# Eight short loads into a scratch tile, between the second and the third chunk of a streaming kernel

## The chip, the cores and the metric

The kernel runs on one core of a Trainium2 chip. The metric is device time in microseconds (us). Each time below is a median of several executions. All executions that were compared carry the label "fast", and the clock granted in them is 1.0 (full speed). A profile covers one execution, and its "span" is some 2 us shorter than the time.

## The reference

```python
# B, S, D = 512, 32, 640; x, fx and alpha are bfloat16, alpha has one element
def reference(x, fx, alpha):
    return x + alpha * fx
```

There is hardly any arithmetic. 41.9 MB have to be read and 21.0 MB written.

## The kernel before

The tensors are seen as 128 partitions of 163840 B each and cut into five chunks of 128 x 16384 elements (4 MB). Each chunk has a load of x, a load of fx, one VectorE (DVE) operation, and a store. All large transfers are issued by SP (SyncE) in the order of the program; alpha is loaded by ACT. A tile framework puts in the semaphores and their waits; the program order is kept as written. A semaphore is a counter that a transfer raises when it has landed, and for which an instruction can wait.

```python
    def load_x(k):
        xt[k] = xs.tile([P, CHUNK], x.dtype, tag="x", name="x_t")      # 4 buffers
        nc.sync.dma_start(out=xt[k][:], in_=xv[:, bass.ts(k, CHUNK)])

    def load_f(k):
        ft[k] = fs.tile([P, CHUNK], fx.dtype, tag="f", name="f_t")     # 2 buffers
        nc.sync.dma_start(out=ft[k][:], in_=fxv[:, bass.ts(k, CHUNK)])
    ...                                # compute(k): x_t = f_t * alpha + x_t on DVE; store(k): x_t to out
    load_x(0)
    load_f(0)
    load_x(1)
    load_f(1)
    load_x(2)
    compute(0)
    load_f(2)
    store(0)
    load_x(3)
    compute(1)
    load_f(3)
    store(1)
    ...                                # on in the same way; the last chunk is computed and stored in halves
```

I write x(k), f(k) and store(k) for the transfers of chunk k.

## Time and profile before

| | before |
|---|---|
| time | 152.69 us (152.47 to 152.9) |
| span of the profiled execution | 150.6 us |
| bytes moved, mean rate | 62.92 MB, 418 GB/s |
| DMA queue 1, share of 16 engines | 98.0% |
| DVE busy | 58% |

These lines are from the page of the kernel before. The "DMA" row gives the busy share of the 16 DMA engines in 40 equal slices of the span, in tenths (9 is 90% or more); the last line gives packets, megabytes and the share of 16 engines' span.

```profile
span 150.6 us, 85 instructions
DVE  0000009999679998499991006999900089997000
DMA  6999999999999999799999999999999999999994
q1 hardware_dynamic: 2304, 62.92, 98.0%
```

The DMA engines have work from the first slice to the last. In the trace nearly every 32 KB packet (one row of a chunk) takes 1.213 us on its engine, and 16 x 32768 B / 1.213 us is 432 GB/s. The Trainium skill, page "DMA: Bandwidth & Descriptors", section "Where 436 GB/s comes from", gives 435 GB/s as the ceiling of the fabric and says that between HBM and SBUF the HBM side, about 358 GB/s, is what binds; the trace fits the first figure and not the second (432 GB/s in the packets, 418 GB/s over the span, with one core at work). DVE keeps waiting for data (49.5 us in all).

The timeline of the kernel before: start, duration (both us), engine, source line, operation, output and input. "SPq" is the issue of a DMA by SP, not the transfer. The brackets give the idle time before an operation and what ended it.

```profile
0.73 0.38 SPq L59 DMA_DIRECT2D x_t<-in_x_dram  x1
2.10 0.57 SPq L63 DMA_DIRECT2D f_t<-in_fx_dram  x1
2.71 0.48 SPq L59 DMA_DIRECT2D x_t<-in_x_dram  x1
22.84 17.28 DVE L69 SCALAR_TENSOR_TENSOR x_t<-f_t,a_f,x_t 128x16384 bf16<-128x16384 bf16 x1 [20.57 <-DMA f_t<-in_fx_dram]
40.16 0.33 SPq L63 DMA_DIRECT2D f_t<-in_fx_dram  x1
42.25 17.28 DVE L69 SCALAR_TENSOR_TENSOR x_t<-f_t,a_f,x_t 128x16384 bf16<-128x16384 bf16 x1 [2.12 <-DMA f_t<-in_fx_dram]
62.24 17.28 DVE L69 SCALAR_TENSOR_TENSOR x_t<-f_t,a_f,x_t 128x16384 bf16<-128x16384 bf16 x1 [2.71 <-DMA f_t<-in_fx_dram]
```

The issue at 2.71 us is x(2): five transfers of 9.7 us each are queued by 3.2 us. The DVE starts mark when f(0), f(1) and f(2) have landed, within a tenth of a us. f(2) is issued at 40.16 us, when the first DVE operation has set its buffer free; x(2) has then not even begun to move, so the queue does not run empty.

### The profile page before, as it was taken

Reading aid. Unit: us, or ns where it says so; the run is one execution under the profiler, and the core shown is the slowest. Engines: PE = TensorE matmul, PEld = TensorE weight load, DVE = VectorE, ACT = ScalarE, POOL = GpSimd, SP = SyncE. Lnnn points to the kernel's source line nnn. Section 1 sums busy time; section 2 is a strip of 40 time slices with the busy share of each in tenths; the row PEclk is TensorE's granted clock in tenths of the full one; section 3 lists DMA queues with packets and bytes.
Section 4 is the critical chain, followed back from the end, with each engine's and each line's share of the span. In section 5 each row is a group of like instructions: output and inputs, shape, how many; then the busy total and the mean of one; then the engine's idle time right before and its main releaser. Section 6 shows DMA issues by size and latency. Waiting matters only on the chain.

```text
span 150.6 us, 85 instructions
## 1 busy us (share of the span) xinstructions
PE 0.2 (0%) x1; PEld 0.1 (0%) x1; DVE 86.9 (58%) x8; POOL 0.2 (0%) x4
## 2 busy tenths in 40 slices
PE   0000000000000000000000000000000000000000
PEld 0000000000000000000000000000000000000000
DVE  0000009999679998499991006999900089997000
POOL 0000000000000000000000000000000000000000
DMA  6999999999999999799999999999999999999994
GB/s 200 444 453 435 418 418 418 418 444 453 444 453 435 418 418 418 339 444 470 418 418 418 418 418 435 435 435 453 426 435 444 418 418 435 435 435 405 426 444 205
DMA packets 2306, 62.92 MB, mean 418 GB/s; under 512 B 258, under 2 KB 258, under 8 KB 258
## 3 DMA queue, kind: packets, MB, share of 16 engines
q1 hardware_dynamic: 2304, 62.92, 98.0%
q10 hardware_dynamic: 2, 0.00, 0.0%
HBM read 41.94 MB, written 20.97 MB: 418 GB/s over the span
## 4 chain that ended last, share of the span: by engine, by line
DMA 56%; DVE 29%; DVEq 6%; issue 0%; SPq 0%
DMA f_t<-in_fx_dram 56%; DVE x_t L69 29%; DVEq L131 6%; SPq L59 0%; DVEq L69 0%
## 5 line engine op out<-in xcount | busy, mean ns | idle before, releaser
L69 DVE SCALAR_TENSOR_TENSOR x_t<-f_t,a_f,x_t 128x16384 bf16<-128x16384 bf16 (+1 forms) x6 | 86.6, 14439 | 49.5 <-DMA f_t<-in_fx_dram 49.5
L26 DVE COPY a_f<-a_ps 128x1 f32<-128x1 f32 x1 | 0.2, 159 | 1.1 <-PE a_ps L24 1.1
L22 DVE MEMSET ones<- 1x128 bf16 x1 | 0.2, 165 | 0.8 <-PEq L120 0.8
L24 PE MATMUL a_ps<-a,ones 1*128 1x1 bf16 x1 | 0.2, 159 | 1.9 <-DMA a<-in_alpha_dram 1.9
L120 POOL MEMSET const-bfloat16-1.0<- 128x1 bf16 x1 | 0.1, 102 | 0.0
L120 POOL MEMSET const-uint8-127<- 128x1 uint8 x1 | 0.1, 102 | 0.0
L24 PEld LDWEIGHTS <-ones 1*128 1x128 bf16 x1 | 0.1, 100 | 1.0 <-DVE ones L22 1.0
L120 POOL MEMSET const-float32-0.0<- 128x1 f32 x1 | 0.1, 99 | 0.2 <-issue 0.2
L120 POOL MEMSET const-float32-1.0<- 128x1 f32 x1 | 0.1, 99 | 0.0
## 6 DMA issues: line engine op xcount, KB each, us to landing
x_t<-in_x_dram SPq DMA_DIRECT2D x5, 4096.0 KB, 34.8
f_t<-in_fx_dram SPq DMA_DIRECT2D x5, 4096.0 KB, 32.1
out_dram<-x_t SPq DMA_DIRECT2D x4, 4096.0 KB, 36.5
out_dram<-x_t SPq DMA_DIRECT2D x2, 2048.0 KB, 15.2
a<-in_alpha_dram ACTq DMA_DIRECT2D x1, 0.0 KB
```

Of the source, the lines that this page charges most:

```text
L22: nc.vector.memset(ones[:], 1.0)
L24: nc.tensor.matmul(a_ps[:], ones[:], a_1[:], start=True, stop=True)
L26: nc.vector.tensor_copy(out=a_f[:], in_=a_ps[:])
L69: nc.vector.scalar_tensor_tensor(out=xt[k][:, s], in0=ft[k][:, s], scalar=a_f[:], in1=xt[k][:, s], op0=ALU.mult, op1=ALU.add,)
L120: nc = _bacc.Bacc("TRN2", target_bir_lowering=False, num_devices=1)
L131: with _tile.TileContext(nc) as tc:
```

## The change

It adds eight loads of 15 down to 2 rows (512 to 736 B each) into a scratch tile that nobody reads. The output is the same.

```diff
     load_x(1)
     load_f(1)
+    m_t = consts.tile([16, 8 * 512], x.dtype, name="m_t")
+    for i, n in enumerate([15, 14, 12, 10, 8, 6, 4, 2]):
+        w = 256 + 16 * i
+        nc.sync.dma_start(out=m_t[:n, i * 512 : i * 512 + w], in_=xv[:n, :w])
     load_x(2)
     compute(0)
     load_f(2)
```

I call the eight loads m0 to m7. The diff does not show which semaphores the framework gives out. The built program's own list of SP's instructions with their waits does (an output of the build, not a profile):

```
L59 DMACopy x_t_77<-in_x_dram 128x16384                            # x(0)
L63 DMACopy f_t_79<-in_fx_dram 128x16384                           # f(0)
L59 DMACopy x_t_81<-in_x_dram 128x16384                            # x(1)
L63 DMACopy f_t_83<-in_fx_dram 128x16384                           # f(1)
L92 DMACopy m_t_85<-in_x_dram 15x256                               # m0
L92 DMACopy m_t_85<-in_x_dram 14x272                               # m1
L92 DMACopy m_t_85<-in_x_dram 12x288                               # m2
L92 DMACopy m_t_85<-in_x_dram 10x304 [waits DMAHW0_49]             # m3: alpha's
L92 DMACopy m_t_85<-in_x_dram 8x320 [waits DMAHW1_49]              # m4: x(0)'s
L92 DMACopy m_t_85<-in_x_dram 6x336 [waits DMAHW2_49]              # m5: f(0)'s
L92 DMACopy m_t_85<-in_x_dram 4x352 [waits DMAHW3_49]              # m6: x(1)'s
L92 DMACopy m_t_85<-in_x_dram 2x368 [waits DMAHW4_49]              # m7: f(1)'s
L59 DMACopy x_t_94<-in_x_dram 128x16384 [waits DMAHW5_49]          # x(2): m0's
```

(The comments are mine.) The DMAs take their completion semaphores in rotation from eight, over SP and ACT together, and an issue waits until the last user of its semaphore is complete. Alpha's load, on ACT, has the first of the eight. In the kernel before, x(2) was the sixth DMA and had no wait.

## The prediction

> **What bounds the kernel now.** DMA bandwidth, from start to end. The page shows 62.92 MB over a span of 150.6 us (418 GB/s), queue 1 busy 98.0% of 16 engines' span. A 32 KB row packet takes 1.213 us in the trace (16 x 32768 B / 1.213 us = 432 GB/s); the 4 MB transfers land every 9.7 us in issue order. DVE is busy 58% and only waits (49.5 us for f_t). The last half store is issued at 138.3 us and lands only at the end, so a backlog stands even there. Whatever leaves the DMA queue empty, or adds bytes, goes into the time whole.
>
> **What the change adds.** Eight loads, 71 rows of 512 to 736 B, about 42 KB: below 0.2 us over 16 engines. Nobody reads the tile. Eight issues of 0.33 to 0.57 us each (SP's issues in the timeline) would be harmless: five 4 MB transfers are queued by 3.2 us, worth 50 us.
>
> **What the change moves.** This is the cost. In the built program the DMAs take their completion semaphores in rotation from eight, and its listing of waits shows that an issue waits for the previous user of its semaphore. Before, x(2) was the sixth DMA and waited for nothing (issued 2.71 us). Now alpha, x(0), f(0), x(1), f(1), m0, m1, m2 take all eight, and m3 to m7 wait for alpha, x(0), f(0), x(1), f(1). m7 waits for f(1), which lands at 42.15 us, and x(2) stands behind m7 on SP (it also waits for m0, which lands just behind f(1)). The Trainium skill, "DMA: Bandwidth & Descriptors", section "Anatomy of one DMA", says that such waits are held by the issuing sequencer, not by the DMA engines; so SP sits until 42.2 us and the DMA queue runs dry behind f(1). Rotation by eight leaves later semaphores as before; later waits on short loads are long satisfied.
>
> **Cost.** m7 is issued at 42.2 (0.35 to 0.5 us), x(2) at about 42.65. From an empty queue x(0) took 12.3 us from issue to landing (0.73 to 13.0: 1.0 us to the first packet, first packets of 1.9 instead of 1.2 us). So x(2) lands at about 54.9 instead of 51.87: +3.0 us. f(2), store(0) and x(3) are issued within 2 us of x(2), and 40 us of transfers are then queued; f(3) is issued at 59.6 as before. No later gap absorbs the shift: nearly all 3.0 us arrive at the end.
>
> **Predicted time:** 155.7 us (+3.0 us, 2.0%), range 154.9 to 156.7 (8 in 10). Faster by over 2%: 1%; within 2%: 52%; slower by over 2%: 47%. It stands on the border.
>
> **What would show it.** The timeline: m4 to m7 issued at about 13, 22.7, 32.4 and 42.2 us, x(2) at 42.6. In the slices, one near 42 us with DMA at 2 to 5 tenths instead of 9. The DMA queue's waits: some 10 us each of short loads on x_t and f_t loads. The first two large DVE operations unmoved (22.84, 42.25), the third at about 65 instead of 62.24, everything after later by about 3 us. DVE busy 86.9 us unchanged.
>
> **What would make it wrong.** A warm queue restarting cheaper than x(0)'s start (+2 us); m0 landing late, or short transfers costing microseconds on engine 0 (+4 us or more); the first store's slow packets near 58 us (up to 1.99 us) changing.

## The result, and the profile after

| | before | after |
|---|---|---|
| time, first pair | 152.69 us (2 runs) | 156.53 us (156.5 to 156.55, 2 runs) |
| ratio, first pair | 1 | 1.0247 (95%: 1.022 to 1.0274) |
| time, second set (run e8_after_again) | 152.63 us (7 runs) | 156.05 us (155.69 to 156.33, 4 runs) |
| ratio, second set | 1 | 1.0196 (95%: 1.0145 to 1.0246) |
| span of the first profile | 150.6 us | 154.7 us |

A ratio is the mean time of one kernel's fast runs over the mean of the other's in the same rounds, so it is not quite the ratio of the medians. The change costs 3.4 to 3.8 us. The first pair lies above the 2% border with its whole interval; in the second set the interval holds 2%, so that set alone doesn't decide. The prediction had put the change on this border, with 155.7 us.

The same lines of the page of the changed kernel:

```profile
span 154.7 us, 93 instructions
DVE  0000009999499994099995003999910069998000
DMA  6999999999689999899999999999999999999993
q1 hardware_dynamic: 2446, 62.96, 96.3%
```

The DMA row has a dip (6 and 8) in the slices from 38.7 to 46.4 us. The row counts a packet in the slice where it starts. So does the view by windows, whose share can therefore exceed 1; its last two figures are the share of the 16 engines and GB/s. From 40 to 44 us, before and after:

```profile
40.00:44.00 4.00, 0.00 (x0) 0.00 (x0) 1.88 (x2) 0.00 (x0) 1.00 1.14 492
40.00:44.00 4.00, 0.00 (x0) 0.00 (x0) 1.89 (x2) 0.00 (x0) 1.00 0.75 240
```

The second, smaller dip (8, near 62 us) stands where the kernel before has its 7: it is there in both kernels.

The timeline of the changed kernel, cut around the issues of m4 to m7 (source line 92) and of what follows:

```profile
13.12 0.27 SPq L92 DMA_DIRECT2D m_t<-in_x_dram  x1
22.83 0.27 SPq L92 DMA_DIRECT2D m_t<-in_x_dram  x1
22.94 17.29 DVE L69 SCALAR_TENSOR_TENSOR x_t<-f_t,a_f,x_t 128x16384 bf16<-128x16384 bf16 x1 [20.48 <-DMA f_t<-in_fx_dram]
32.55 0.25 SPq L92 DMA_DIRECT2D m_t<-in_x_dram  x1
42.26 0.23 SPq L92 DMA_DIRECT2D m_t<-in_x_dram  x1
42.34 17.28 DVE L69 SCALAR_TENSOR_TENSOR x_t<-f_t,a_f,x_t 128x16384 bf16<-128x16384 bf16 x1 [2.11 <-DMA f_t<-in_fx_dram]
42.54 0.36 SPq L59 DMA_DIRECT2D x_t<-in_x_dram  x1
43.01 0.36 SPq L63 DMA_DIRECT2D f_t<-in_fx_dram  x1
65.92 17.29 DVE L69 SCALAR_TENSOR_TENSOR x_t<-f_t,a_f,x_t 128x16384 bf16<-128x16384 bf16 x1 [6.30 <-DMA f_t<-in_fx_dram]
```

m4 to m7 leave one by one as x(0), f(0), x(1) and f(1) land. x(2) is issued at 42.54 us instead of 2.71. Its own wait would have held it nearly as long: m0, whose semaphore it takes, was queued behind f(1) and landed only at 42.43 us (39.7 us after its issue), and m7's issue ended at 42.49 us. The runs don't tell these two waits apart; both end just behind f(1). The first two DVE operations have not moved by more than 0.1 us, and the third starts 3.68 us later (65.92 against 62.24). The waits of the DMA queue say the same (issuer, line, what it waited for: us in total, times, longest); first the changed kernel:

```profile
SPq L92 <- DMA f_t<-in_fx_dram: 18.9, 2, 9.4
SPq L92 <- DMA x_t<-in_x_dram: 18.1, 2, 9.4
```

The longest waits of SP in the kernel before were longer than these. They came with 4 MB transfers still queued on the engines:

```profile
SPq L80 <- DVE x_t L69: 55.5, 3, 28.7
SPq L63 <- DVE x_t L69: 41.6, 3, 17.4
SPq L63 <- DMA f_t<-in_fx_dram: 20.2, 2, 19.5
```

A long wait of SP is no loss in itself. It becomes one when the engines run out of what SP has issued already. The chain of work that ended last (start, duration, what) shows this for the changed kernel:

```profile
2.11 40.14 DMA f_t<-in_fx_dram
...
42.26 0.23 SPq L92
42.49 0.04 issue
42.54 0.36 SPq L59
...
43.01 22.82 DMA f_t<-in_fx_dram
```

Between two loads the chain now runs over SP's issue of a load that nobody needs (L92) and the issue of x(2) (L59). In the kernel before, SP appeared in this chain once, at the start; over the same stretch it ran

```profile
22.84 17.30 DVE x_t L69
...
40.16 21.99 DMA f_t<-in_fx_dram
...
62.24 17.29 DVE x_t L69
```

### Where the microseconds are

From the packets' starts and durations in the trace I add up, for each of the 16 engines on average: the time in which no large packet runs, and the time by which large packets exceed 1.213 us (0.611 us for the half rows of the last stores). "Again" is the second profile of each kernel, from the runs e9_before_again and e8_after_again.

| us per engine | before | before again | after | after again |
|---|---|---|---|---|
| idle behind f(1), 40 to 44 us | 0 | 0 | 2.28 | 2.24 |
| slower packets, 40 to 50 us | 0.01 | 0.01 | 0.71 | 0.63 |
| slower packets, 50 to 70 us (before the first store) | 0.88 | 0.81 | 1.27 | 1.39 |
| idle at the end, behind the first engine that is done | 0.42 | 0.95 | 0.97 | 1.04 |
| span | 150.6 | 151.1 | 154.7 | 154.5 |

For the first pair the differences of the four rows add up to 2.28 + 0.70 + 0.39 + 0.55 = 3.92 of the 4.1 us. For the second pair they are 2.24 + 0.62 + 0.58 + 0.09 = 3.53, against 3.3 us of span (there the start of the changed kernel happened to be 0.2 us quicker). The dry stretch and the restart make up 2.9 to 3.0 us in both. The 71 short packets themselves take 27 to 34 ns each in the first profile.

### The profile page after: what moved, and what is told of

Same layout as the page of the kernel before. It is cut to its first block, busy times and chain, and to the rows that moved or that the text cites. A ratio compares the mean times of both kernels' runs of the same rounds, so it can differ in the third digit from the quotient of the medians.

```text
span 154.7 us, 93 instructions
## 1 busy us (share of the span) xinstructions
PE 0.2 (0%) x1; PEld 0.1 (0%) x1; DVE 86.9 (56%) x8; POOL 0.2 (0%) x4
## 4 chain that ended last, share of the span: by engine, by line
DMA 68%; DVE 17%; DVEq 6%; SPq 1%; issue 0%
DMA f_t<-in_fx_dram 68%; DVE x_t L69 17%; DVEq L135 6%; SPq L59 1%; SPq L63 0%; SPq L92 0%; DVEq L69 0%
## 6 DMA issues: line engine op xcount, KB each, us to landing
x_t<-in_x_dram SPq DMA_DIRECT2D x5, 4096.0 KB, 12.3
m_t<-in_x_dram SPq DMA_DIRECT2D x1, 7.5 KB, 39.7
```

## The experiments

Theory A: SP stands still. m7 needs the semaphore of f(1), x(2) is held behind m7, the DMA engines finish f(1) with nothing queued, and a restart from empty costs about 3 us. Rival B: the short rows themselves cost, by their small packets or by their uneven load of the 16 engines. Rival C: eight more issues on SP cost. Eleven runs were made, two of them repeats, all with a correct result.

| run | what it is | time, us | ratio (95%) | third DVE start, us |
|---|---|---|---|---|
| e1_act_queue | the eight loads issued by ACT | 153.07 | 1.0042 (0.9984 to 1.01) | 62.34 |
| e2_six | first six of them | 152.4 | 1.0008 (0.9948 to 1.0068) | 63.26 |
| e3_seven | first seven | 155.9 | 1.0212 (1.0185 to 1.0239) | 65.97 |
| e4_rows16 | eight, all of 16 rows | 156.74 | 1.0257 (1.0227 to 1.0287) | 66.00 |
| e5_one_dry | none; one copy that waits for f(1) | 157.33 | 1.0279 (1.0206 to 1.0352) | 66.36 |
| e6_behind_x2 | eight, behind x(2) | 156.44 | 1.0217 (1.0159 to 1.0276) | 66.30 |
| e7_first | eight, ahead of everything | 155.72 | 1.0178 (1.0127 to 1.0229) | 65.29 |
| e8_after_again | the change again | 156.05 | 1.0196 (1.0145 to 1.0246) | 65.78 |
| e9_before_again | the kernel before again | 152.8 | 0.999 (0.9955 to 1.0025) | 62.44 |
| e10_six16 | six, all of 16 rows | 152.57 | 0.9985 (0.9951 to 1.0018) | 62.56 |
| e11_dry_then_six | the one copy, then six behind x(2) | 157.04 | 1.0269 (1.0222 to 1.0316) | 65.89 |

The kernel before had a median of 152.63 to 152.72 us in these three sets. Single executions of some kernels came out about 1.5 us above the rest of their runs (154.33 us in e2_six, 154.46 us in e1_act_queue, 154.04 us of the kernel before), which widens those intervals.

### The same loads from ACT's queue

```diff
-        nc.sync.dma_start(out=m_t[:n, i * 512 : i * 512 + w], in_=xv[:n, :w])
+        nc.scalar.dma_start(out=m_t[:n, i * 512 : i * 512 + w], in_=xv[:n, :w])
```

> The same eight short loads, issued from ACT's queue. Theory A (the loss is SP standing still: m7 waits for the semaphore of f(1), and x(2) is held behind it, so the DMA queue runs dry near 42 us): SP is not held, x(2) is issued before 20 us, no dip near 42 us, time 152.4 to 153.2 us (the before time). Rival B (the short rows themselves cost, by their small packets or by the uneven load of the 16 engines): the rows are still there, so 155.5 to 157 us. Rival C (eight more issues on SP): also about 152.7, but C is told from A by the six-loads run.

Measured: 153.07 us, not to be told from the kernel before. Its issues in the timeline (ACTq is ACT's queue), and the DMA row of its page:

```profile
1.27 12.48 ACTq L92 DMA_DIRECT2D m_t<-in_x_dram  x8
8.19 0.33 SPq L63 DMA_DIRECT2D f_t<-in_fx_dram  x1
10.72 0.33 SPq L59 DMA_DIRECT2D x_t<-in_x_dram  x1
13.31 0.33 SPq L63 DMA_DIRECT2D f_t<-in_fx_dram  x1
14.49 0.33 SPq L59 DMA_DIRECT2D x_t<-in_x_dram  x1
DMA  6999999999999999999999999999999999999993
```

The rows are all there, and no dip. SP is not free of waits here either: f(0) to x(2) still stand behind short loads' semaphores, since the rotation is shared by SP and ACT; in the built program ACT's eight loads take their semaphores before f(0) does. But the last of them is issued at 14.49 us, and each came while an earlier 4 MB transfer still ran. So these waits on recycled semaphores cost nothing measurable while the queue held work. B, as the cause of 3.8 us, falls.

### Six and seven of the loads

```diff
-    for i, n in enumerate([15, 14, 12, 10, 8, 6, 4, 2]):
+    for i, n in enumerate([15, 14, 12, 10, 8, 6]):        # e2_six; e3_seven has [15, 14, 12, 10, 8, 6, 4]
```

> Only the first six short loads. In the built program the last waits for f(0) (22.7 us) and x(2) for x(1) (32.4 us), so x(2) is issued at about 32.5 us with f(1) still to run. Theory A: never dry, 152.4 to 153.3 us. B and C: in proportion to the loads, six eighths of +3.8 us, about 155.5 us.

> The first seven short loads. Now x(2) itself takes the semaphore of f(1) and waits until 42.2 us. Theory A: a step up from six loads, x(2) issued at 42.2 instead of 42.54 us, so 156.2 us, about 0.3 below the change itself. B and C: seven eighths of +3.8 us, about 156.0, and only 0.5 us above six loads.

Measured: 152.4 and 155.9 us. One load of 4 rows (704 B each) makes a step of 3.5 us, and no cost by the load, the byte or the issue can do that. The issue of x(2) and the DMA row, first with six loads:

```profile
32.49 0.36 SPq L59 DMA_DIRECT2D x_t<-in_x_dram  x1
DMA  6999999999999999999999999999999999998990
```

and with seven:

```profile
42.38 0.36 SPq L59 DMA_DIRECT2D x_t<-in_x_dram  x1
DMA  6999999999689999899999999999999999999993
```

With six loads x(2) inherits the semaphore of x(1) and leaves 10 us before f(1) is through; with seven it inherits that of f(1) itself and leaves too late. B and C had expected 155.5 us for six loads. (The profiled execution with six loads is the one of 154.33 us: there one engine's last landing was 1.3 us late, which is the 0 at the end of its row. The other three were 152.27 to 152.46 us.)

### Eight loads of 16 rows

```diff
-    for i, n in enumerate([15, 14, 12, 10, 8, 6, 4, 2]):
+    for i, n in enumerate([16, 16, 16, 16, 16, 16, 16, 16]):
```

> Eight short loads again, but all of 16 rows, so that each of the 16 engines gets the same rows. Theory A: semaphores and waits as in the change, 156.2 to 156.7 us. Rival B in its form of uneven engines: the loss, or at least the growth of the spread between the engines' last landings (0.8 us before, 1.5 us after), goes away, 152.7 to 155.8 us.

Measured: 156.74 us. Neither the row counts nor an uneven load of the engines matter for the loss. The spread of the last landings was 0.95 us here, which at this point looked like a gain; the repeats below take that back.

### A dry queue without any short load

```diff
-    for i, n in enumerate([15, 14, 12, 10, 8, 6, 4, 2]):
-        w = 256 + 16 * i
-        nc.sync.dma_start(out=m_t[:n, i * 512 : i * 512 + w], in_=xv[:n, :w])
+    nc.sync.dma_start(out=m_t[:16, :256], in_=ft[1][:16, :256])
     load_x(2)
```

> No short load at all. One copy of 16 rows of 512 B from the tile of f(1) to the scratch tile stands on SP before x(2); it needs f(1)'s data, so SP waits for f(1) until 42.2 us as in the change. Theory A (an empty DMA queue behind f(1), whatever empties it): x(2) issued at about 42.6 us, time 155.6 to 156.8 us, with the slower packets near 62 us and the wider spread of the last landings there as well if they follow from the restart. Rival B (the short loads): 152.4 to 153.2 us.

Measured: 157.33 us in the median, though its four runs lie far apart (156.29 to 158.3). The issues in its timeline, and the DMA row:

```profile
42.17 0.57 SPq L90 DMA_DIRECT2D m_t<-f_t  x1
42.78 0.58 SPq L59 DMA_DIRECT2D x_t<-in_x_dram  x1
DMA  7999999999579999999999999999999999999994
```

That is above the 155.6 to 156.8 us that theory A expected. No short load from memory, and no recycled semaphore ahead of x(2): one copy that really needs f(1) makes the same dip, and a loss at least as large (3.7 us in the profiled execution, the fastest of the four; 4.7 us in the median). The dry stretch alone is enough. Its idle time is 2.95 us per engine instead of 2.28 us, since the copy takes longer to issue and x(2) starts later. Why the other three executions took up to 2 us more is not shown; they have no profile.

### The loads one place later

```diff
     load_f(1)
+    load_x(2)
     m_t = consts.tile([16, 8 * 512], x.dtype, name="m_t")
     ...
-    load_x(2)
     compute(0)
```

> The eight short loads one place later, behind x(2). The last now takes the semaphore of x(2), so SP stands until x(2) lands (51.9 us) and f(2) is issued at 52.2 instead of 40.16 us. Theory A: the dip in the DMA slices moves from 42 to 52 us; x(2) lands as before, f(2) about 3 us later; time 155.5 to 156.8 us. Were it x(2)'s late issue alone that costs, 152.7 us.

Measured: 156.44 us. Issue of f(2), and the DMA row:

```profile
52.27 0.36 SPq L63 DMA_DIRECT2D f_t<-in_fx_dram  x1
DMA  7999999999999599899999999999999999999993
```

The dip has moved from the slices near 42 us to the one near 52 us, because the last load now inherits x(2)'s semaphore. The loss stayed the same size.

### The loads ahead of everything

```diff
+    m_t = consts.tile([16, 8 * 512], x.dtype, name="m_t")
+    ...                                       # the same eight loads
     load_x(0)
     load_f(0)
     load_x(1)
     load_f(1)
-    ...
     load_x(2)
```

> The eight short loads ahead of everything, where SP's issue time is exposed since nothing is queued yet. Eight issues of 0.3 to 0.5 us put x(0)'s issue from 0.73 to 3.4 to 4.3 us, and the time to 155.3 to 156.4 us: that is what eight issues are worth at most. The waits on earlier semaphores are short there (alpha, the first short load). No dip near 42 us.

Measured: 155.72 us. The timeline:

```profile
0.72 2.92 SPq L88 DMA_DIRECT2D m_t<-in_x_dram  x8
3.69 0.36 SPq L59 DMA_DIRECT2D x_t<-in_x_dram  x1
```

Where nothing is queued, eight issues cost what they last: 2.96 us later for x(0), and 3.09 us in time (155.72 against 152.63). That is nearly as much as the change costs, so the size alone would not have told theory C from A. The place does: in the changed kernel the first four issues fall into the first 5 us under a full queue, and m4 to m6 under f(0), x(1) and f(1); only m7's 0.23 us lies in the dry stretch.

### The repeats, and what was left over

The 3.0 us of dry stretch and restart leave 0.4 to 0.8 us. Two terms showed in the table of packets: slower packets before the first store, and a wider spread of the 16 engines' last landings (0.79 us before, 1.47 us after). Four runs looked at them: repeats of both kernels, six even loads, and

```diff
-    for i, n in enumerate([15, 14, 12, 10, 8, 6, 4, 2]):        # e11_dry_then_six
+    nc.sync.dma_start(out=m_t[:16, 3584:3840], in_=ft[1][:16, :256])
+    load_x(2)
+    for i, n in enumerate([15, 14, 12, 10, 8, 6]):
         w = 256 + 16 * i
         nc.sync.dma_start(out=m_t[:n, i * 512 : i * 512 + w], in_=xv[:n, :w])
-    load_x(2)
```

e10_six16 has the loop over `[16] * 6` in the place that the change has it.

> The changed kernel once more, for a second profile and an interval. 156.3 to 156.8 us. If the slower packets near 62 us (1.27 us in sum for each engine in the first profile, 0.88 in the kernel before) and the spread of the last landings (1.5 us) are properties of the change, they come back within 0.2 us; if they are chance, they don't.

> The kernel before once more, for a second profile: 152.4 to 153.0 us. If the slower packets at the first store (0.88 us summed for each engine in the first profile, against 1.2 to 1.4 us in the five kernels whose queue ran dry) are a property of the kernel, 0.7 to 1.0 us again.

> Six short loads as in the six-loads run, but each of 16 rows, the same for every engine. Never dry: 152.4 to 153.2 us. Unevenness theory of the spread: the last landings of the engines lie within 0.7 to 1.0 us, not 1.4 us or more. Step theory of the slower packets at the first store (engines that run in step disturb each other more there): 0.8 to 1.0 us for each engine, not the 0.5 of six uneven loads. If neither shows, both are chance.

> One copy makes the queue dry behind f(1) as in the one-copy run, x(2) follows, and six uneven short loads stand behind x(2), so the engines are out of step from 55 us on. The dry stretch stays: x(2) lands 3.0 to 3.4 us late. Step theory of the slower packets at the first store: their sum falls from 1.35 to 0.4 to 0.9 us, and the time to 155.4 to 156.3 us. Rival (the sum is larger after a dry stretch for another reason): 1.2 to 1.4 us again, time 156.3 to 157 us.

Measured: 156.05, 152.8, 152.57 and 157.04 us. The repeat of the change lies below the 156.3 us that I had expected at least. With packets summed as above:

| | slower packets 50 to 70 us | spread of the last landings, us |
|---|---|---|
| before, before again | 0.88, 0.81 | 0.79, 1.48 |
| after, after again | 1.27, 1.39 | 1.47, 1.39 |
| seven loads; eight of 16 rows; one copy (all dry behind f(1)) | 1.40; 1.18; 1.35 | 1.68; 0.95; 0.79 |
| six loads; six of 16 rows (never dry) | 0.50; 0.06 | 2.73; 1.48 |
| loads by ACT; loads ahead of everything (no dry stretch behind f(1)) | 0.41; 0.88 | 1.45; 1.12 |
| one copy, then six behind x(2) | 0.88 | 1.23 |

The spread is no property of the change: the kernel before has 0.79 us in one execution and 1.48 us in the next. By the test that I had set for e8_after_again it would have passed for one (1.39 us came back within 0.2 us of 1.47); the repeat of the kernel before was needed to see that it isn't. My unevenness theory of it fell with e9_before_again and e10_six16.

The slower packets do not look like chance, though each figure is of one execution. All five profiles with a queue that ran dry behind f(1) and nothing else behind x(2) have 1.18 to 1.40 us, and those of the kernel before 0.81 and 0.88: 0.3 to 0.6 us of the loss. The other four without such a dry stretch have 0.06 to 0.88 us. e6_behind_x2, dry at 52 us, has 1.52 us from 58 to 66 us alone, where the kernel before has 0.85 and 0.78. My theory that engines in step disturb each other fell too: six even loads should have given 0.8 to 1.0 us and gave 0.06. There, 0.57 us of slower packets stood between 40 and 50 us instead, behind the short rows, where the kernel before has 0.01, so the sum over both stretches was 0.63 us against 0.89 us, with 0.2 us of idle engines added, and the time did not change. e11_dry_then_six is inconclusive: its 0.88 (of which 0.28 stand at 54 to 58 us, beside the short rows) lies in the range that the step theory expected, but its time, 157.04 us, lies above it, and in that kernel store(0) was issued only at 55.49 us, because it waits for a recycled semaphore as well (x(2)'s). What makes packets slow shortly before the first store, and more so after a dry stretch, stays open.

No version beat the kernel before. Of those that keep all eight loads, issuing them from ACT is the one that costs nothing measurable.

## Why the prediction was right or wrong

- **The bound: right.** The queue was full throughout, and what left it empty went into the time whole.
- **The eight semaphores and the chain to f(1): right.** m4 to m7 were forecast for about 13, 22.7, 32.4 and 42.2 us and left at 13.12, 22.83, 32.55 and 42.26 us. x(2) was forecast for about 42.65 and left at 42.54 us. The step between six and seven loads (152.4 to 155.9 us) and the dip that moves with the place of the loads show that it is this wait; the run with one copy shows that the dry queue alone is enough.
- **The cost of the restart: right in the first pair, and from the right source.** x(0) took 12.3 us from issue to landing at the kernel's start; x(2) in the changed kernel was issued at 42.54 us and landed at 54.81 us by its semaphore, again 12.3 us, 2.9 us later than before (51.87 us). In the second pair it took 12.0 us and landed 2.4 us later (54.43 against 52.02 us); a landing is that of the slowest engine, and the mean over the engines is the 2.9 us of the table above. The first packets were slow again: 1.65 to 2.39 us on 15 of the 16 engines at the restart, 1.62 to 2.40 us on all 16 at the start. A warm queue restarted hardly cheaper.
- **That a wait is held by the sequencer: right.** The prediction took this from the Trainium skill, "DMA: Bandwidth & Descriptors", section "Anatomy of one DMA", which describes DMAs issued from GpSimd but says it of the DMA engines in general. The trace agrees for SP: the issues behind m7 did not leave before 42.5 us, and the engines that had f(1) still to do worked on.
- **"Nearly all 3.0 us arrive at the end": right as far as it went, and too small.** The measured loss is 3.84 us in the first pair and 3.42 us in the second set. The mis-sized term is the first store's slow packets, which the sum took as unchanged (the prediction named it among what would make it wrong). It measured 0.3 to 0.6 us more after the dry stretch. The rest, up to half a us in the first pair, goes with the spread of the last landings, which varies as much between two executions of the kernel before.
- **The dip in the slices: half right.** One slice of 2 to 5 tenths was forecast; it was 6 and 8. A slice lasts 3.87 us, and the 2.3 us fall into two of them.
- **Waits of "some 10 us each": right**, the longest are 9.4 us. DVE's busy time did not change (86.9 us), and f(3) was issued at 59.65 us, as forecast (59.6).
- **m7's issue: a little too dear.** 0.35 to 0.5 us were forecast and 0.23 us measured; it made little difference.

## What to carry to other kernels

Count, in the built program, the DMAs that stand between a transfer and the last earlier one that shares its completion semaphore: a transfer that must be issued early to keep the queue full may be held by an unrelated one, or by a trifle issued ahead of it on the same sequencer. What such a wait costs is not its length (here 37 us of waits on loads in all) but the time in which the queue is empty plus a restart, some 3 us here, and one more or one less short transfer can switch that on or off. Keep small transfers off the queue that feeds the large ones, or below the number at which the wait reaches the last transfer in flight. Another issuing engine is no full escape, since the rotation is shared: with the short loads on ACT, f(0) left at 8.19 us instead of 1.16, and that cost nothing measurable while x(0) was still moving.

## What the Trainium skill lacked or had wrong

- "DMA: Bandwidth & Descriptors", section "Specifications", gives about 0.6 us to the first byte for DMAs issued from SP. From the start of the issue to the first packet, the trace shows 1.0 us both at the start (0.73 to 1.74 us) and at the restart (42.54 to 43.52 us). The measurement decides for this kind of transfer; where the page's interval starts is not said there.
- No page gives what a drained queue of large transfers costs. Here: 2.3 us of idle engines from the end of f(1) to the first packet of x(2), plus 0.7 us because the first packets took 1.65 to 2.39 instead of 1.213 us on 15 of the 16 engines.
- The same page warns about sharing one semaphore between DMAs in flight ("Why a DMA increments its semaphore by 16 and not by 1"), but no page says what avoiding that by waiting costs: reuse of eight semaphores made a load of 4 rows cost 3.5 us (six loads against seven).
- The same page, section "Rules for kernel authors", says that issuing from several engines "only saves sequencer issue time"; it speaks of bandwidth and leaves out the waits. Here moving the eight loads from SP to ACT took 156.05 to 156.53 us back to 153.07 us, since it also freed the large loads from standing behind a waiting small one.
- No page has the slower packets shortly before the first store behind loads: up to 1.99 and 2.09 us instead of 1.213 us in the two profiles of the kernel before, 0.88 and 0.81 us per engine in sum. The cause is open.
